# Hedgehog attention plus gated MLP on one core: transposes by DMA in place of TensorE, and a reordered start

## The chip, the cores and the metric

The kernel runs on one core of a Trainium2 chip. The metric is device time in microseconds (us). The core has five engines that run side by side: TensorE (PE, matmuls), VectorE (DVE), ScalarE (ACT), GpSimd (POOL) and SyncE (SP), which here only issues DMA transfers. Matmul results land in PSUM, a small memory of eight banks, and an engine has to copy ("evict") them to SBUF, the on-chip working memory, before they can be a matmul's input again.

## The reference: what is computed

The input x has 2048 rows of 640 in bf16. It is layer-normed once. Two branches use the result and are added to x: a linear attention with 32 heads of 20 columns whose feature map is a softmax of plus and minus a projected q or k ("hedgehog"), and a gated MLP of width 1536.

```python
def _A_ref(x, wqkv, w_phi, wo):
    qkv = (x @ wqkv) ...                              # q, k, v: 32 heads of 20
    pq = jnp.einsum("bhsd,hdf->bhsf", q, w_phi)
    pk = jnp.einsum("bhsd,hdf->bhsf", k, w_phi)
    phi_q = concat([softmax(pq), softmax(-pq)])       # phi_k the same from pk
    kv = jnp.einsum("bhsf,bhsd->bhfd", phi_k, v)
    z  = jnp.einsum("bhsf->bhf", phi_k)
    num = jnp.einsum("bhqf,bhfd->bhqd", phi_q, kv)
    den = jnp.einsum("bhqf,bhf->bhq", phi_q, z)[..., None] + 1e-6
    return (num / den) ... @ wo
def _B_ref(x, w1, w3, w2):
    h = silu(x @ w1) * (x @ w3)
    return h @ w2
xn = _layernorm(x)
return x + _A_ref(xn, ...) + _B_ref(xn, ...)
```

## The kernel before

The 2048 rows are 16 tiles of 128 rows, or 4 chunks of 512. A small planner (`Plan`) takes the operations in the order in which the code lists them, assigns each a guessed duration, and writes out the program in the order of its simulated start. The steps are:

- **LN and T(t)**: layer norm of tile t on DVE, then five PE transposes into a PSUM bank and an evicting copy to `xnT` (columns of x on the partitions).
- **V(t)**, **K(t)**: projections of tile t, ten matmuls of 320 columns each; for K two exponentials (plus and minus), row sums, reciprocal and the two products `phik`.
- **prep**: folds the feature map's weights into wk and wq (`wkphi`, `wqphi`), after transposing these weights on PE.
- **KV(t)**: accumulates kv and z over all tiles in two PSUM banks, `kva` and `kvb`.
- **GU(c, fi)**: one 128-wide slice of gate and up for a chunk (five matmuls of 512 columns each), tanh on ACT, the product `gs` on DVE, and the product `hT` on DVE or on POOL. These units are used as filler between the other steps (`fill`).
- **Q(c, g)**, **RT(t)**, **ATT(pair)**: q for a chunk, numerators and denominators, and the attention output `om` of two tiles.
- **OT(t)** and **O(t)**: transposes `om` on PE, then multiplies hT by w2 and oT by wo into one bank; the residual is added as the bank is evicted.

```python
# ... (cut)
for t in range(4):
    load_x(t, 1)
nc.sync.dma_start(out=wv[:], in_=wqkv3[:, :, 2 * D : 3 * D])
load_gu(0)
nc.sync.dma_start(out=wk[:], in_=wqkv3[:, :, D : 2 * D])
load_x(4, 4)
load_gu(1)
load_x(8, 4)
load_gu(2)
load_gu(3)
nc.sync.dma_start(out=wq[:], in_=wqkv3[:, :, 0:D])
nc.sync.dma_start(out=w2[:], in_=B_w2.rearrange("(c p) d -> p c d", p=P))
# ... (cut)
def T(t, evac="DVE"):
    ln_apply(t)
    # ...
        for c in range(KD):
            nc.tensor.transpose(o["ps"][:, c * P : (c + 1) * P], box["t"][:, c * P : (c + 1) * P], ident[:])
    # ... and the copy
            nc.vector.tensor_copy(out=dst, in_=src)
# ... (cut) prep: transposes, copy, product with wphi
                    for c in range(KD):
                        nc.tensor.transpose(
                            box["ps"][:gw, c * P : (c + 1) * P], src[:, c, 120 * g : 120 * g + gw], ident[:]
                        )
                nc.vector.tensor_copy(out=box["wT"][:gw, :], in_=box["ps"][:gw, :])
                            nc.tensor.matmul(
                                o["ps"][:, c - c0, 0:gw], box["wT"][:gw, c * P : (c + 1) * P], wphi[:gw, g, 0:gw]
                            )
# ... (cut) OT
        for c in range(KD):
            nc.tensor.transpose(o["ps"][:, c * P : (c + 1) * P], box["om", 0][...][:, c * P : (c + 1) * P], ident[:])
        nc.vector.tensor_copy(out=o["oT"][:], in_=o["ps"][:].rearrange("p (c s) -> p c s", c=KD))
# ... (cut) which engine makes hT
def modes(n):
    return "DVE" if n % 3 == 0 else "POOL"
# ... (cut) the second half
RT(0); RT(1); ATT(0); fill(2.2)
for i in range(NST // 2):
    nxt = i + 1
    # RT, ATT of pair nxt, a fill, Q of the next chunk
    OT(2 * i); OT(2 * i + 1)
    O(2 * i); O(2 * i + 1)
```

Of the kernel before, what the change touches and what calls it, by code (L numbers as in the profile page):

```python
# [8 lines left out]
P = 128  # L9


class Plan:
# [7 lines left out]
    def op(self, eng, dur, fn, deps=(), takes=None, frees=(), after=0.0):  # L20
        o = dict(eng=eng, dur=dur, fn=fn, deps=[d for d in deps if d is not None], takes=takes,
                 frees=list(frees), after=after, n=len(self.ops), end=None, open=0)
        for f in o["frees"]:
            f["open"] += 1
        self.ops.append(o)
        return o
# [4 lines left out]
    def run(self):  # L31
# [20 lines left out]
        while left:  # L52
# [14 lines left out]
            o["start"], o["end"] = t, t + o["dur"]  # L67
            free[o["eng"]] = o["end"]
# [7 lines left out]
        for o in out:  # L76
            o["fn"]()
# [3 lines left out]
def kernel(  # L81
# [22 lines left out]
    H = 32  # L104
# [6 lines left out]
    NG = 6  # L111
    GW = [120] * 5 + [40]
    GH = [6] * 5 + [2]
    NQ = 5
    HC = 22
# [16 lines left out]
    xpool = ctx.enter_context(tc.tile_pool(name="xpool", bufs=3))  # L132
    wv, wk, wq = (big.tile([P, KD, D], bf, name=n, tag="big") for n in ("wv", "wk", "wq"))
    xg = {}
    w1 = wpool.tile([P, KD, F], bf, name="w1")
# [4 lines left out]
    wphi = consts.tile([P, NG, P], bf, name="wphi")  # L140
# [5 lines left out]
    kva = kvpool.tile([P, 512], f32, name="kva")  # L146
    kvb = kvpool.tile([P, 512], f32, name="kvb")
# [4 lines left out]
    def load_x(t0, n):  # L152
        i, k = t0 % 4, t0 // 4
        if i == 0:
            xg[k] = xpool.tile([P, 4, D], bf, name="xg", tag="xg")
        nc.sync.dma_start(
            out=xg[k][:, i : i + n, :],
            in_=x2[t0 * P : (t0 + n) * P, :].rearrange("(t p) d -> p t d", p=P),
        )

    def xt(t):
        return xg[t // 4][:, t % 4, :]
# [5 lines left out]
    for t in range(4):  # L168
        load_x(t, 1)
    nc.sync.dma_start(out=wv[:], in_=wqkv3[:, :, 2 * D : 3 * D])  # L170
    load_gu(0)
    nc.sync.dma_start(out=wk[:], in_=wqkv3[:, :, D : 2 * D])
    load_x(4, 4)
    load_gu(1)
    load_x(8, 4)
    load_gu(2)
    load_gu(3)
    nc.sync.dma_start(out=wq[:], in_=wqkv3[:, :, 0:D])
    nc.sync.dma_start(out=w2[:], in_=B_w2.rearrange("(c p) d -> p c d", p=P))

    nc.vector.memset(wphi[:], 0.0)
    for hh in range(6):
        n = len(range(hh, H, 6))
        nc.scalar.dma_start(
            out=wphi[Dh * hh : Dh * hh + Dh, 0:n, Dh * hh : Dh * hh + Dh],
            in_=A_w_phi[hh:H:6].rearrange("g j f -> j g f"),
        )
    ident = consts.tile([P, P], bf, name="ident")
    make_identity(nc, ident[:])
    eps = consts.tile([P, 1], f32, name="eps")  # L190
    nc.vector.memset(eps[:], EPS)
    mhalf = consts.tile([P, NST], f32, name="mhalf")
    nc.vector.memset(mhalf[:], -0.5)
    for v in vaug:
        nc.gpsimd.memset(v[:, :, Dh : Dh + 1], 1.0)

    band = consts.tile([P, 20], bf, name="band")
    nc.gpsimd.memset(band[:], 1.0)
    for lo in (0, 64):
        rows = band[lo : lo + 64, :]  # L200
        nc.gpsimd.affine_select(
            out=rows, in_=rows, pattern=[[-4, 20]], base=16, channel_multiplier=1,
            compare_op=ALU.is_ge, fill=0.0,
        )
        nc.gpsimd.affine_select(
            out=rows, in_=rows, pattern=[[4, 20]], base=3, channel_multiplier=-1,
            compare_op=ALU.is_ge, fill=0.0,
        )
    mask = consts.tile([P, 10, 4], bf, name="mask")
    for j in range(10):  # L210
        b = 4 - (64 * j - Dh * h0[j]) // 4
        nc.gpsimd.tensor_copy(out=mask[:, j, :], in_=band[:, b : b + 16 : 5])
    for kv in kvr:
        nc.gpsimd.memset(kv[:], 0.0)
# [6 lines left out]
    for kv in kvr:  # L221
        for g in range(NQ):
            lo, hi = halves(kv, g)
            nc.gpsimd.tensor_copy(out=lo[:, :, HC - 1], in_=mask[0:64, 2 * g, :])
            nc.gpsimd.tensor_copy(out=hi[:, :, HC - 1], in_=mask[64:128, 2 * g + 1, :])

    plan = Plan(dict(bank=6, row=4, half=2, pair=4, rt=4, th=3, gs=3, up=3, hT=3, big=4, xg=3))
# [13 lines left out]
    arrive = [3.2, 3.6, 4.0, 4.4] + [13.0] * 4 + [19.0] * 8  # L241
    rstd_of = {}
    X_of = {k: plan.alloc("xg", lambda: None) for k in range(3)}
    X_of[3] = plan.op("SP", 0.5, lambda: load_x(12, 4), takes="xg")
    xg_of = dict(X_of)
    big_of = {n: plan.alloc("big", lambda: None) for n in ("wv", "wk", "wq")}
    xn_of = {}
    T_of = {}

    def ln_stats(t):  # L250
        def fn():
            for i in range(2):
                nc.vector.bn_stats(out=stats[:, t, i, :], in_=xt(t)[:, i * 320 : (i + 1) * 320])  # L253
            nc.vector.bn_aggr(out=mv[:, t, :], in_=stats[:, t, :, :])

        return plan.op("DVE", 0.9, fn, after=arrive[t], deps=[X_of.get(t // 4)])

    def ln_rstd(t0, n, pool):
        ds = [ln_stats(t) for t in range(t0, t0 + n)]
        if pool:  # L260

            def fn():
                v = small.tile([P, n], f32, name="vareps", tag=f"vareps{n}")
                nc.gpsimd.tensor_scalar_add(v[:], mv[:, t0 : t0 + n, 1], EPS)
                nc.gpsimd.tensor_tensor(
                    out=rstd[:, t0 : t0 + n], in0=v[:], in1=mhalf[:, 0:n], op=ALU.pow
                )

            r = plan.op("POOL", 1.5, fn, deps=ds)
        else:  # L270

            def fn():
                nc.scalar.activation(
                    out=rstd[:, t0 : t0 + n], in_=mv[:, t0 : t0 + n, 1], func=AF.Sqrt,
                    bias=eps[:, 0:1], scale=1.0,
                )

            a = plan.op("ACT", 0.3, fn, deps=ds)
            r = plan.op(
                "DVE", 0.1,  # L280
                lambda: nc.vector.reciprocal(out=rstd[:, t0 : t0 + n], in_=rstd[:, t0 : t0 + n]),
                deps=[a],
            )
        for t in range(t0, t0 + n):
            rstd_of[t] = r

    def ln_apply(t):
        box = {}

        def al():  # L290
            box["t"] = work.tile([P, D], bf, name="xn", tag="row", bufs=4)

        a = plan.alloc("row", al)

        def fn():
            nc.vector.tensor_scalar(
                out=box["t"][:], in0=xt(t), scalar1=mv[:, t, 0:1], scalar2=rstd[:, t : t + 1],
                op0=ALU.subtract, op1=ALU.mult,
            )

        xn_of[t] = (plan.op("DVE", dve_us(D, 4), fn, deps=[rstd_of[t], a], frees=[xg_of[t // 4]]), a, box)
# [4 lines left out]
    def T(t, evac="DVE"):  # L306
        ln_apply(t)
        dep, xb, box = xn_of[t]
        o = {}

        def fn():
            o["ps"] = bank([P, D], bf)
            for c in range(KD):
                nc.tensor.transpose(o["ps"][:, c * P : (c + 1) * P], box["t"][:, c * P : (c + 1) * P], ident[:])

        u = plan.op("PE", pe_us(KD, P), fn, deps=[dep], takes="bank", frees=[xb])
# [9 lines left out]
        T_of[t] = plan.op(evac, dve_us(D, 2) if evac == "DVE" else act_us(D), ev, deps=[u], frees=[u])  # L326
# [16 lines left out]
    def V(t):  # L343
        V_of[t] = []
        for half in range(2):
            u, o = proj(t, wv, half, [T_of[t]], [big_of["wv"]])
# [11 lines left out]
    def K(t):  # L358
# [11 lines left out]
        for half in range(2):  # L370
            u, o = proj(t, wkphi, half, [T_of[t]] + wphi_ready["k"])
# [10 lines left out]
        def red():  # L382
            box["s"] = small.tile([P, 2, H], f32, name="ks", tag="ks")
# [7 lines left out]
        def rec():  # L391
            box["r"] = small.tile([P, 2, H], f32, name="kr", tag="kr")
            nc.vector.reciprocal(out=box["r"][:], in_=box["s"][:])  # L393
# [3 lines left out]
        def mul(sgn):  # L397
            def fn():
                eng = nc.vector if sgn == 0 else nc.gpsimd
                eng.tensor_mul(  # L400
# [25 lines left out]
    def prep(key, src, dst, after):  # L426
        wphi_ready[key] = []
        units = []
        for g in range(NG):
            gw = GW[g]  # L430
            box = {}

            def tr(g=g, gw=gw, box=box):
                def fn():
                    box["ps"] = bank([P, D], bf)
                    for c in range(KD):
                        nc.tensor.transpose(
                            box["ps"][:gw, c * P : (c + 1) * P], src[:, c, 120 * g : 120 * g + gw], ident[:]
                        )

                def al():
                    box["wT"] = work.tile([P, D], bf, name="wT", tag="half", bufs=2)

                box["al"] = plan.alloc("half", al)
                u = plan.op("PE", pe_us(KD, P), fn, takes="bank", after=after, frees=[big_of["w" + key]])

                def ev():
# [417 lines left out]
```

The softmax here doesn't subtract the row's maximum and nothing guards it: scores larger than these inputs give would overflow.

## Time and profile before

| | before |
|---|---|
| device time, median of 4 runs | 307.31 us (306.32 to 307.86) |
| span of the profiled run | 306.1 us |
| first matmul starts | 7.39 us |
| loads in the first 40 us | about 300 GB/s on average, then almost none |
| HBM read, written | 14.44 MB, 2.62 MB |

How to read it: the page gives busy time by engine, the span in 40 slices (each digit is the busy share of a slice in tenths), and the chain of work that ended last, followed back from the end. Rows of groups name the line, the engine, the operation, "output<-inputs", the shape and the count. An engine's idle time is put down to what released it. A PE that is shown as busy need not run at its peak, because matmuls overlap; their true pace is seen from start to start in the timeline. Some matmul records are missing from the trace, so a count in a row can be a few per cent below the program's.

### The profile page before, as it was taken

The numbers are of one execution on the slowest core, as the hardware profiler recorded it, in microseconds if no ns is written. First come the engines' busy times: TensorE is split into PE (matmuls) and PEld (weight loads), VectorE is DVE, ScalarE is ACT, GpSimd is POOL, SyncE is SP. The second block draws the span as 40 slices with busy tenths as digits, with TensorE's granted clock in tenths as the row PEclk, the third lists the DMA queues.
The fourth block names the chain that finished last, engine by engine and source line by source line (L and its number), as shares of the span: only waits on it lengthen the run. The fifth ranks groups of instructions, "written<-read, shape, count | busy, mean of one in ns | idle before, by whom it ended". The sixth has DMA issues, their size and how long they took to land.

```text
span 306.1 us, 5207 instructions
## 1 busy us (share of the span) xinstructions
PE 282.0 (92%) x2053; PEld 175.3 (57%) x2076; DVE 198.3 (65%) x349; ACT 140.9 (46%) x309; POOL 74.6 (24%) x101
## 2 busy tenths in 40 slices
PE   0768999969999999999999999999998999999995
PEld 0434555526655666656545476665765657657773
DVE  6269699988888776686656944738247372681931
ACT  4135565525555655656488815057060480631100
POOL 8213243253424333354310300011012020120000
PEclk9999999979999999999999999999999999999999
DMA  7999800020003000000300000030000100001011
GB/s 201 349 336 351 290 3 1 0 86 1 0 2 86 2 0 2 2 2 0 109 0 2 0 21 24 6 122 4 22 24 11 34 0 24 21 0 36 9 45 43
DMA packets 16723, 17.39 MB, mean 57 GB/s; under 512 B 1340, under 2 KB 16700, under 8 KB 16700
## 3 DMA queue, kind: packets, MB, share of 16 engines
q1 hardware_dynamic: 16000, 17.04, 17.3%
q8 instruction: 16, 0.26, 0.3%
q10 hardware_dynamic: 700, 0.03, 0.2%
q14 instruction: 7, 0.06, 0.1%
HBM read 14.44 MB, written 2.62 MB: 56 GB/s over the span
## 4 chain that ended last, share of the span: by engine, by line
PE 67%; DVE 16%; issue 6%; DMA 5%; ACT 5%; SPq 1%; POOL 0%; POOLq 0%
PE bank L502 24%; PE bank L738 13%; PE bank L336 10%; PE bank L742 6%; PE bank L590 6%; DVE stats L253 3%; ACT rt L641 3%; DVE gs L523 2%; DMA wv<-in_A_wqkv_dram 2%; DMA xg<-in_A_x_dram 2%; PE bank L633 2%; DVE ks L384 2%; ACT eq L605 2%; DVE phik L400 2%; PE bank L709 1%
## 5 line engine op out<-in xcount | busy, mean ns | idle before, releaser
L502 PE MATMUL bank<-xnT,w 128*128 128x512 bf16 x457 | 109.8, 382 | 5.2 <-DVE xnT L322 2.9
L502 PEld LDWEIGHTS <-w 128*128 128x128 bf16 x480 | 46.9, 98 | 56.0 <-issue 7.1
L545 POOL TENSOR_TENSOR hT<-gs,up 128x512 bf16<-128x512 bf16 x32 | 38.1, 1192 | 157.2 <-DVE gs L523 81.1
L738 PE MATMUL bank<-w,hT 128*128 128x320 bf16 x384 | 57.4, 299 | 0.0
L641 ACT CAST rt<-bank 128x352 bf16<-128x352 f32 x64 | 23.6, 496 | 56.5 <-PE bank L633 47.6
L738 PEld LDWEIGHTS <-hT 128*128 128x128 bf16 x384 | 37.3, 98 | 14.3
L747 DVE TENSOR_TENSOR res<-bank,xg 128x320 bf16<-128x320 f32 x32 | 15.7, 491 | 43.4 <-PE bank L742 43.4
L518 ACT ACTIVATE th<-bank 128x512 bf16<-128x512 f32 x48 | 29.2, 608 | 28.8 <-PE bank L502 27.2
L336 PEld LDWEIGHTS <-xnT 128*128 128x128 bf16 x320 | 30.5, 99 | 19.4 <-DVE xnT L322 5.3
L523 DVE SCALAR_TENSOR_TENSOR gs<-th,bank 128x512 bf16<-128x512 bf16 x48 | 32.3, 675 | 6.7 <-ACT th L518 6.7
L384 DVE TENSOR_REDUCE ks<-ek 128x64 f32<-128x1280 bf16 x16 | 23.7, 1482 | 17.2 <-ACT ek L375 17.2
L400 POOL TENSOR_TENSOR phik<-ek,kr 128x640 bf16<-128x640 bf16 x16 | 24.4, 1528 | 26.0 <-DVE kr L393 23.6
L336 PE MATMUL bank<-wv,xnT 128*128 128x320 bf16 x160 | 25.7, 310 | 5.1 <-DVE xnT L322 3.5
L742 PE MATMUL bank<-wo,oT 128*128 128x320 bf16 x160 | 27.0, 299 | 1.8 <-DVE oT L718 1.8
L375 ACT ACTIVATE ek<-bank 128x320 bf16<-128x320 f32 x64 | 23.1, 435 | 9.3 <-PE bank L336 9.2
L540 ACT ACTIVATE up<-bank 128x512 bf16<-128x512 f32 x32 | 19.1, 597 | 16.8 <-PE bank L502 16.8
L400 DVE TENSOR_TENSOR phik<-ek,kr 128x640 bf16<-128x640 bf16 x16 | 24.6, 1539 | 0.2
L336 PE MATMUL bank<-wkphi,xnT 128*128 128x320 bf16 x160 | 24.4, 299 | 0.0
L349 ACT CAST vaug<-bank 128x320 bf16<-128x320 f32 x32 | 13.7, 428 | 22.0 <-PE bank L336 21.9
L605 ACT ACTIVATE eq<-bank 128x512 bf16<-128x512 f32 x40 | 21.6, 594 | 3.2 <-PE bank L590 3.2
L590 PE MATMUL bank<-xnT,wqphi 128*128 128x512 bf16 x100 | 22.2, 379 | 0.0
L742 PEld LDWEIGHTS <-oT 128*128 128x128 bf16 x160 | 15.5, 98 | 8.4 <-DVE oT L718 2.4
(61 smaller groups left out, 244.1 us busy)
## 6 DMA issues: line engine op xcount, KB each, us to landing
xg<-in_A_x_dram SPq DMA_DIRECT2D x7, 640.0 KB, 7.0
w<-in_B_w_dram SPq DMA_DIRECT2D x8, 480.0 KB, 7.9
out_dram<-res SPq DMA_DIRECT2D x16, 160.0 KB, 1.8
w<-in_B_w_dram SPq DMA_DIRECT2D x1, 1920.0 KB
wv<-in_A_wqkv_dram SPq DMA_DIRECT2D x1, 800.0 KB, 7.1
wk<-in_A_wqkv_dram SPq DMA_DIRECT2D x1, 800.0 KB
wq<-in_A_wqkv_dram SPq DMA_DIRECT2D x1, 800.0 KB, 8.8
wo<-in_A_wo_dram SPq DMA_DIRECT2D x1, 800.0 KB, 4.6
```

What stands on the lines that cost most here:

```text
L336: nc.tensor.matmul(o["ps"][:], xnT[:, c, t * P : (t + 1) * P], w[:, c, 320 * half : 320 * half + 320], start=(c == 0), stop=(c == KD - 1),)
L384: nc.vector.reduce_sum(out=box["s"][:].rearrange("p a h -> p (a h)"), in_=box["ek"][:].rearrange("p a (h d) -> p (a h) d", d=Dh), axis=AX.X,)
L400: eng.tensor_mul(out=phik_b[t][:, :, sgn, :], in0=box["ek"][:, sgn, :].rearrange("p (h d) -> p h d", d=Dh), in1=box["r"][:, sgn, :, None]. ...
L502: nc.tensor.matmul(o["ps"][:], w[:, k, fi * P : (fi + 1) * P], xs[:, k, :], start=(k == 0), stop=(k == KD - 1))
L518: nc.scalar.activation(out=box["th"][:], in_=og["ps"][:], func=AF.Tanh, scale=0.5)
L523: nc.vector.scalar_tensor_tensor(out=box["gs"][:], in0=box["th"][:], scalar=1.0, in1=og["ps"][:], op0=ALU.add, op1=ALU.mult)
L545: lambda: nc.gpsimd.tensor_mul(out=hT[c][:, fi, :], in0=box["gs"][:], in1=box["up"][:]),
L590: nc.tensor.matmul(o["ps"][:], wqphi[:, k, g * P : (g + 1) * P], xnT[:, k, c * 512 : (c + 1) * 512], start=(k == 0), stop=(k == KD - 1),)
L605: nc.scalar.activation(out=eqt[c, sgn][:, g, 0:512], in_=o["ps"][:], func=AF.Exp, scale=1.0 - 2.0 * sgn)
L641: nc.scalar.copy(out=rtt[pair, sgn][:, i, 16 * side : 16 * side + 16, :].rearrange("p h c -> p (h c)"), in_=o["ps"][:],)
L738: nc.tensor.matmul(o["ps"][:], hT[c][:, fi, ti * P : (ti + 1) * P], w2[:, fi, cols], start=(fi == 0), stop=False)
L742: nc.tensor.matmul(o["ps"][:], oo["oT"][:, k, :], wo_of[0][:, k, cols], start=False, stop=(k == KD - 1))
```

## The change

It does several things together.

1. The transposes of xn for chunks 1 to 3, of the k and q weights, and of the attention output are made by DMA (`dma_start_transpose`) and no longer by PE with an evicting copy. [...] xn of a chunk and the attention output of a pair are first stored to a scratch tensor there; the weights are read straight from the input.
2. The start is reordered: x tile by tile with wv in halves between, layer norm per tile, two of the four `xnT` copies on ACT, and the prologue's order fixed by hand. Ten dummy matmuls on zeros (`warm`) run while PE waits for the first data.
3. The phi weights are loaded with one DMA and spread over the block diagonal on POOL; the folding writes three matmuls into one 320-column bank.
4. The product `hT` is on POOL for the first 36 gate/up units, and on DVE for every third after that.
5. x for the residual is loaded again into its own buffers; xn, x, oT and the residual share one pool of four.
6. The attention pairs run two ahead of O instead of one, and half of RT's banks are the two that KV had used.

```diff
@@ loads at the start
+        for t in range(4):
+            load_x(xg[0], t, 1, 0)
+            if t < 2:
+                nc.sync.dma_start(
+                    out=wv[:, :, 320 * t : 320 * t + 320],
+                    in_=wqkv3[:, :, 2 * D + 320 * t : 2 * D + 320 * t + 320],
+                )
+        load_gu(0)
+        load_x(xg[1], 0, 4, 1)
+        nc.sync.dma_start_transpose(out=wkT[:], in_=A_wqkv[:, D : 2 * D])
+        for i in range(1, 4):
+            load_gu(i)
... (cut)
+    def warm():
+        nc.vector.memset(xnT[:, 0, 0:512], 0.0)
+        ps = bank([P, 512], f32)
+        for i in range(WARM):
+            nc.tensor.matmul(ps[:], xnT[:, 0, 0:P], xnT[:, 0, 0:512])
+    WARM = 10
... (cut) layer norm of chunks 1 to 3
+        st = plan.op(
+            "SP", 0.5,
+            lambda: nc.sync.dma_start(out=xn_d[c][:].rearrange("(t p) d -> p t d", p=P), in_=xn[c][:]),
+            deps=ds, frees=[a], lat=3.5,
+        )
+        xt = plan.op(
+            "SP", 0.5,
+            lambda: nc.sync.dma_start_transpose(out=xnT[:, :, 512 * c : 512 * c + 512], in_=xn_d[c][:]),
+            deps=[st], lat=5.0,
+        )
... (cut) prep
-                        nc.tensor.transpose(
-                            box["ps"][:gw, c * P : (c + 1) * P], src[:, c, 120 * g : 120 * g + gw], ident[:]
-                        )
-                    nc.vector.tensor_copy(out=box["wT"][:gw, :], in_=box["ps"][:gw, :])
+                    for n, (g, at, width, col) in enumerate(FSPANS[side]):
+                        nc.tensor.matmul(
+                            o["ps"][:, at : at + width], wT[:, g, c * P : (c + 1) * P],
+                            wphi[:, g, :, :].rearrange("p i f -> p (i f)")[:, col : col + width], ...
... (cut) OT
-                nc.tensor.transpose(o["ps"][:, c * P : (c + 1) * P], box["om", 0]..., ident[:])
-            nc.vector.tensor_copy(out=o["oT"][:], in_=o["ps"][:].rearrange("p (c s) -> p c s", c=KD))
+            lambda: nc.sync.dma_start(
+                out=o_d[pair][:].rearrange("(t p) d -> p t d", p=P),
+                in_=box["om", 0][:].rearrange("p (t h) d -> p t (h d)", t=2),
+            ),
+            deps=[dep], frees=[ob], lat=2.5,
+            lambda: nc.sync.dma_start_transpose(out=oT[c][:, :, 256 * i : 256 * i + 256], in_=o_d[pair][:]),
+            deps=[st, oT_a[c]], lat=3.5,
... (cut)
     def modes(n):
-        return "DVE" if n % 3 == 0 else "POOL"
+        return "DVE" if n % 3 == 0 and n >= 36 else "POOL"
... (cut) after the start; wqT and w2 are held back to these times of the plan
+    plan.op("SP", 0.5, lambda: nc.sync.dma_start_transpose(out=wqT[:], in_=A_wqkv[:, 0:D]), after=24.0)
+    LN(1)
+    plan.op("SP", 0.5, lambda: nc.sync.dma_start(out=w2[:], ...), after=36.0)
... (cut) the second half
+    residual(0)
+    attend(0, 2.2)
+    attend(1, 2.2)
     for i in range(NST // 2):
-        nxt = i + 1
+        nxt = i + 2
```

## The prediction, made before the changed kernel ran

> **What bounds the kernel now.** I read the busy line and the 40 slices first, to see which engine fills the span and where it doesn't.
>
> ```profile
> PE 282.0 (92%) x2053; PEld 175.3 (57%) x2076; DVE 198.3 (65%) x349; ACT 140.9 (46%) x309; POOL 74.6 (24%) x101
> PE   0768999969999999999999999999998999999995
> DVE  6269699988888776686656944738247372681931
> ```
>
> TensorE (PE) is at 9 in nearly every slice after the fifth. So the kernel is a stream of matmuls with a slow start, and two questions remain: how dense that stream is, and what the start costs. Next, the timeline of PE alone over the first 22 us (start, duration, count, and in brackets the idle time before):
>
> ```profile
> 7.39 0.71 PE L314 MATMUL bank<-ident,xn 128*128 128x128 bf16 x5 [7.39 <-DVE xn L296]
> 9.75 2.82 PE L336 MATMUL bank<-wv,xnT 128*128 128x320 bf16 x10 [1.65 <-DMA wv<-in_A_wqkv_dram]
> 13.69 1.53 PE L336 MATMUL bank<-wv,xnT 128*128 128x320 bf16 x10 [0.59 <-DVE xnT L322]
> 17.69 1.53 PE L336 MATMUL bank<-wv,xnT 128*128 128x320 bf16 x10 [2.19 <-DVE xnT L322]
> 20.20 1.53 PE L336 MATMUL bank<-wv,xnT 128*128 128x320 bf16 x10 [0.69 <-DVE xnT L322]
> 21.57 4.48 PE L502 MATMUL bank<-xnT,w 128*128 128x512 bf16 x19
> ```
>
> The gate/up matmuls (L502) begin only at 21.57 us. Until then PE has done four transposes of five and four V projections of ten; it waited for layer norm, for wv, and for the copies of xnT. The first V group takes 2.82 us and the later ones 1.53.
>
> The table by stage (columns: stretch, its length, then busy us and count for PE, PEld, DVE, ACT, POOL, then PE clock, DMA share, GB/s) shows the middle:
>
> ```profile
> 40.00:65.00 25.00, 21.79 (x149) 12.55 (x150) 24.46 (x34) 13.89 (x33) 11.48 (x11) 0.98 0.01 1
> 65.00:154.00 89.00, 88.38 (x670) 54.08 (x681) 66.39 (x83) 50.42 (x115) 34.80 (x27) 0.99 0.08 25
> 154.00:303.00 149.00, 145.99 (x1062) 93.41 (x1066) 81.24 (x161) 59.85 (x130) 13.55 (x11) 1.00 0.07 22
> ```
>
> From 40 to 65 us VectorE (DVE) is busy 24.46 of 25: there it is the bound. The chain of work that ended last says the same; from 38 to 64 us it runs mostly over DVE:
>
> ```profile
> 42.24 1.49 DVE ks L384
> 43.73 0.59 DVE gs L523
> 44.70 0.63 DVE hT L532
> 45.33 1.55 DVE phik L400
> ```
>
> After 65 us PE is full. In the waits of PE only two lines belong there:
>
> ```profile
> PE bank L502 <- DVE xnT L322: 2.9, 1, 2.9
> PE bank L742 <- DVE oT L718: 1.8, 2, 1.2
> ```
>
> **What the Trainium skill says.** "TensorE: Matmul & The Clock Gate", section "Back-to-back issue gap", gives about N/2.4 + 2.5 ns per warm matmul of N columns. The trace agrees: the timeline has 10 matmuls of 512 in 2.16 us (216 ns each), 10 of 320 in 1.36, 10 transposes of 128 in 0.56. Section "What's actually happening" says the clock is halved until the array has been busy for some 3.4 us; the first V group at 2.82 us against 1.53 fits that. "DMA: Bandwidth & Descriptors", section "Latency and other measured facts", gives 261 GB/s for one transposing DMA; no such DMA is in this trace. "VectorE: DVE Perf Modes", section "The three transpose paths", gives 1309 ns for one 128x128 block by DMA against 390 on TensorE. If the blocks ran one after another that would be 25 GB/s. These two disagree tenfold in what they imply; this is my main uncertainty.
>
> **PE's work, counted.** From the program, by the trace's pace: 580 matmuls of 512 x 0.216 = 125.3 us; 864 of 320 x 0.136 = 117.5; 220 transposes x 0.056 = 12.3; 60 for folding phi x 0.054 = 3.2; 192 of the attention (24 in 1.40 us, 0.058) = 11.2; 160 of kv x 0.038 = 6.1. Sum 275.6 of 306.1. The other 30.5 us: 7.4 before the first matmul; 3.3 after the last (302.84 to 306.1); and about 20 in between, which I place with the counted work of each stretch: some 14 before 65 us, 6 after.
>
> **The change, part by part.**
> 1. *Transposes leave PE.* Tiles 4 to 15 of xn (12 x 5), both weights (60) and the attention output (80) now go by DMA: 200 x 0.056 = 11.2 us off PE, all of it inside a full stream, so I count it fully. The folding of phi stays at 60 matmuls of the same mean width: 0. PE's work becomes 264.4 us, not counting the ten warming matmuls.
> 2. *The start.* x arrives tile by tile with wv in halves between, layer norm goes per tile, and ScalarE takes two of the four xnT copies. DVE per tile: stats 0.86, reciprocal 0.13, apply 0.40 (0.80 for two), and two copies of 0.47 in all; from 2.93 us, when x arrives, that is 4 x 1.39 + 0.94 = 6.5, plus about 0.5 for hops: xnT of tile 3 at about 10 us. V(2) and V(3) follow, so gate/up starts at about 12.7 instead of 21.57. PE's work up to there is the same 6.6 us, so 8.9 us are saved. Ten dummy matmuls from 1.3 us fill the wait and take the cold pace (2.82 - 1.53 = 1.3 us) off the first group; this is inside the 8.9.
> 3. *DVE is relieved* in the stretch where it bounds: 14 of 16 copies of xnT go (12 with their transposes, 2 to ScalarE; 14 x 0.48 = 6.7), 12 wT copies (5.6), 12 of 16 hT products go to POOL (12 x 0.65 = 7.8), and later 16 oT copies (7.1). DVE goes from 198 to about 171. From gate/up's start to the last K tile I count for DVE 32 gs x 0.675 + 16 x (1.48 + 0.54 + 1.54) + 12 stats x 1.05 + 12 applies x 0.6 = 98 us, beside PE's 32 x 2.16 + 16 K and 12 V x 1.36 + 16 kv x 0.38 + 3.2 = 116: DVE is no longer the bound, though at 85% it still makes PE wait here and there. ACT takes 12 more up copies (7.2) and POOL 12 x 1.19 = 14.3; both are under 60%. Of the 14 us lost from 7.4 to 65 us about 7.5 fall before 21.57 (14.2 less 6.6 of work), which part 2 covers, and 6.5 after; I let 4 remain.
> 4. *New waits.* xn of a chunk is stored to DRAM, then read back transposed. The plan's own figures are 3.5 + 5 us for 640 KB and 2.5 + 3.5 for 320 KB. For chunk 1: apply ends near 21 us; the queue then still holds about 2 MB of weights (loads ran at 345 GB/s), store lands near 29, transpose near 37. PE needs it after 12 gate/up units and four K: 12.7 + 12 x 2.16 + 3.2 / 2 + 4 x 1.36 + 0.8 = 46. Hidden with 9 us to spare. wkT: about 3 MB lie ahead of it, so it starts near 11.5 us and lands near 15; PE asks at 12.7 + 3 x 2.16 = 19.2. Hidden. For the first attention output: from the last matmul of tile 1 to the use, PE has two gate/up units, six attention groups of 0.84 less two, one Q of 5.4 and 12 matmuls: 4.3 + 3.4 + 5.4 + 1.6 = 14.7 us. The chain is rt copies 2, coefficients 2.1, products and sum 3.9, a gs 0.7, store and transpose 6, hops 1: 15.7. About 1 us of stall. The two waits above (2.9, 1.8) go away.
>
> Sum: 264.4 work + 6.1 before gate/up (12.7 - 6.6) + 4 to 65 us + 4 after + 3.3 tail = 281.8. I add 3 us for transposing DMAs slower than the plan's figures and for waits in SP's queue, which is in order. The timed median is about 1.2 over the profiled span (307.31 against 306.1). Together: 286 us.
>
> **Rivals.**
> - *The transposing DMA is slow.* At 100 GB/s (8 us for 800 KB) wkT and the second weight chunk come 2 us late and chunk 1 about 2: near 290. At 25 to 50 GB/s wkT would land at 28 or later, the weights queued behind it with it, and xn of chunk 1 some 10 us late: 304 to 315. Against it: the one stated bandwidth, and the plan's figures. For it: the 1309 ns.
> - *DVE stays the bound to 140 us.* If the 1.5 us products and reductions grow further because POOL now has 44 instead of 32 multiplications beside them, the K stage runs at DVE's pace: 98 us x 1.18 = 116, as much as PE has; order waits would then cost some 5 to 8 us, giving 291 to 294.
> - *SP's queue blocks.* Stores, transposes, residual loads and output stores stand in one order, and each issue waits for its own producer. An output store waiting for DVE in front of a transpose would show as PE waiting on oT; 1 to 2 us a time, four times, near 291.
> - *All hidden, better start.* Gate/up from 11.5 us and hardly a wait: 278.
>
> **Range and chances.** 278 is the hidden case, 297 holds the milder rivals together. Slower than 301 needs a really slow transpose. 278 to 297; faster 0.91, same 0.06, slower 0.03.
>
> **What will show it.** Right: no L314-style transposes on PE but 20; first gate/up near 12.7 us; DVE under 90% from 40 to 65; PE's waits on DMA xnT, wkT and oT under 3 us in total; transposing DMAs landing in 3 to 6 us. Wrong: PE waiting on DMA wkT or xnT for many us (first rival); PE waiting on DVE gs or phik through the K stage (second); PE waiting on oT at each pair (third).

## The result, and the profile after

The changed kernel takes 281.72 us (median; 280.72 to 284.24), the kernel before 307.84 in the same series: ratio 0.9169, 95% interval 0.9143 to 0.9194. (The ratio is taken over all runs and is not the quotient of the two medians.) The prediction was 286.0 with a range of 278 to 297.

The page of the changed kernel, busy line and slices:

```profile
PE 269.6 (97%) x1862; PEld 163.3 (58%) x1886; DVE 172.5 (62%) x295; ACT 145.9 (52%) x320; POOL 95.7 (34%) x124
PE   6799999999999999999999999999999999999994
DVE  4683789979767666857629976223664706647221
```

PE is at 9 from the third slice on, and no 8 is left in the middle. Its first 6 is mostly the dummy matmuls, so "97% busy" flatters it a little. The timeline of PE over the start:

```profile
1.24 4.18 PE L210 MATMUL bank<-xnT 128*128 128x512 bf16 x10 [1.24 <-DVE xnT L207]
5.55 0.45 PE L377 MATMUL bank<-ident,xn 128*128 128x128 bf16 x5
7.00 1.53 PE L399 MATMUL bank<-wv,xnT 128*128 128x320 bf16 x10 [1.01 <-DVE xnT L385]
9.37 0.45 PE L377 MATMUL bank<-ident,xn 128*128 128x128 bf16 x5 [0.84 <-DVE xn L327]
...
12.58 2.89 PE L399 MATMUL bank<-wv,xnT 128*128 128x320 bf16 x20
15.30 6.64 PE L548 MATMUL bank<-xnT,w 128*128 128x512 bf16 x29
```

Gate/up (L548) begins at 15.30 us, against 21.57 before. The first V group takes 1.53 us instead of 2.82, as every later one does. The table by stage, with the same columns as before:

```profile
40.00:65.00 25.00, 24.84 (x168) 14.22 (x170) 23.14 (x36) 15.41 (x33) 16.20 (x14) 1.00 0.36 122
65.00:140.00 75.00, 74.12 (x531) 44.07 (x539) 53.02 (x85) 50.47 (x112) 42.00 (x31) 1.00 0.18 47
140.00:276.00 136.00, 134.81 (x954) 85.61 (x960) 70.71 (x123) 55.18 (x123) 13.14 (x11) 1.00 0.24 67
```

From 40 to 65 us PE is now busy 24.84 of 25 (21.79 before). DVE still has 23.14, but PE no longer waits for it. The waits of PE over the whole span, less the four of the start (3.8 us together), are two lines:

```profile
PE bank L548 <- DVE gs L569: 0.4, 1, 0.4
PE rtbank L682 <- ACT rt L690: 0.2, 1, 0.2
```

No DMA stands among them. Only the weight loads (PEld), which overlap PE, waited 0.4 us for one, a transposed attention output (the last entry of the row):

```profile
L794 PEld LDWEIGHTS <-oT 128*128 128x128 bf16 x160 | 15.5, 98 | 6.4 <-DMA oT<-od 0.4
```

All transposing transfers of this kernel read DRAM: the scratch tensors `xnd` and `od`, and the weights in the input. Here they are with the stores in front of them, in the DMA view (count, size if given, median us from issue to landing):

```profile
od<-om SPq DMA_DIRECT2D x8, 320.0 KB, 2.3
xnd<-xn SPq DMA_DIRECT2D x3, 640.0 KB, 3.2
...
oT<-od SPq DMA_TRANSPOSE x8, 3.6
xnT<-xnd SPq DMA_TRANSPOSE x3, 4.8
...
wkT<-in_A_wqkv_dram SPq DMA_TRANSPOSE x1, 9.7
wqT<-in_A_wqkv_dram SPq DMA_TRANSPOSE x1, 10.6
```

**Where the time went.** By the prediction's count PE's work is 275.6 us before and 264.4 after, so 30.5 us of the span before (306.1) and 14.8 of the span after (279.2) are without work. The balance closes on the span's 26.9 us:

| us | before | after | change |
|---|---|---|---|
| PE's counted work | 275.6 | 264.4 | -11.2 |
| without work ahead of gate/up (start of gate/up less 6.6 of work) | 15.0 | 8.7 | -6.3 |
| without work between that and the last matmul (the rest) | 12.2 | 2.5 | -9.7 |
| after the last matmul (302.8 and 275.6) | 3.3 | 3.6 | +0.3 |

Of the 9.7 us, 6.0 are waits: PE's list before names 6.6 us after the start of gate/up (2.9, 1.8, 0.9, 0.8 and 0.2), the list now 0.6. Another 1.3 us went by at a low clock behind the longest of these waits; the section on the rule for hT shows it. The rest is not placed.

The balance says where time was saved, not which part of the change saved it. The experiments undo one part at a time.

### The profile page after: what moved, and what is told of

Same layout as the page of the kernel before. It is cut to its first block, busy times and chain, and to the rows that moved or that the text cites. A ratio compares the mean times of both kernels' runs of the same rounds, so it can differ in the third digit from the quotient of the medians.

```text
span 279.2 us, 4872 instructions
## 1 busy us (share of the span) xinstructions
PE 269.6 (97%) x1862; PEld 163.3 (58%) x1886; DVE 172.5 (62%) x295; ACT 145.9 (52%) x320; POOL 95.7 (34%) x124
## 2 busy tenths in 40 slices
DMA packets 44614, 26.54 MB, mean 95 GB/s; under 512 B 26288, under 2 KB 44592, under 8 KB 44592
## 4 chain that ended last, share of the span: by engine, by line
PE 85%; issue 4%; ACT 4%; DVE 2%; DMA 2%; POOL 1%; SPq 1%; ACTq 0%; POOLq 0%
PE bank L548 35%; PE bank L790 17%; PE bank L399 14%; PE bank L794 7%; PE bank L636 6%; PE rtbank L682 2%; DMA xg<-in_A_x_dram 2%; ACT eq L651 2%; PE bank L682 2%; PE bank L505 1%; PE kva L481 1%; PE kvb L481 1%; ACT rt L690 1%; POOL phik L464 1%; DVE xn L327 1%
## 5 line engine op out<-in xcount | busy, mean ns | idle before, releaser
L548 PE MATMUL bank<-xnT,w 128*128 128x512 bf16 x460 | 109.7, 379 | 1.5 <-DVE gs L569 0.4
L591 POOL TENSOR_TENSOR hT<-gs,up 128x512 bf16<-128x512 bf16 x44 | 51.3, 1166 | 141.7 <-ACT up L586 84.0
L548 PEld LDWEIGHTS <-w 128*128 128x128 bf16 x480 | 46.3, 98 | 49.4 <-issue 0.7
L790 PE MATMUL bank<-w,hT 128*128 128x320 bf16 x384 | 58.1, 299 | 0.0
L586 ACT ACTIVATE up<-bank 128x512 bf16<-128x512 f32 x44 | 26.3, 597 | 23.3 <-PE bank L548 21.7
L447 DVE TENSOR_REDUCE ks<-ek 128x64 f32<-128x1280 bf16 x16 | 23.6, 1475 | 17.4 <-ACT ek L438 17.4
L464 POOL TENSOR_TENSOR phik<-ek,kr 128x640 bf16<-128x640 bf16 x16 | 29.7, 1856 | 5.5 <-ACT th L564 5.5
L799 DVE TENSOR_TENSOR res<-bank,xr 128x320 bf16<-128x320 f32 x32 | 15.5, 486 | 25.4 <-PE bank L794 25.4
L690 ACT CAST rt<-bank 128x352 bf16<-128x352 f32 x32 | 13.1, 469 | 26.4 <-PE bank L682 18.8
L399 PE MATMUL bank<-wv,xnT 128*128 128x320 bf16 x160 | 24.4, 299 | 1.8 <-DVE xnT L385 1.0
L464 DVE TENSOR_TENSOR phik<-ek,kr 128x640 bf16<-128x640 bf16 x16 | 21.9, 1366 | 1.4
L636 PEld LDWEIGHTS <-wqphi 128*128 128x128 bf16 x100 | 9.6, 98 | 10.8
```

The source lines that it names most:

```text
L399: nc.tensor.matmul(o["ps"][:], xnT[:, c, t * P : (t + 1) * P], w[:, c, 320 * half : 320 * half + 320], start=(c == 0), stop=(c == KD - 1),)
L447: nc.vector.reduce_sum(out=box["s"][:].rearrange("p a h -> p (a h)"), in_=box["ek"][:].rearrange("p a (h d) -> p (a h) d", d=Dh), axis=AX.X,)
L464: phik_ins[t] = eng.tensor_mul(out=phik_b[t][:, :, sgn, :], in0=box["ek"][:, sgn, :].rearrange("p (h d) -> p h d", d=Dh), in1=box["r"][:, ...
L548: nc.tensor.matmul(o["ps"][:], w[:, k, fi * P : (fi + 1) * P], xs[:, k, :], start=(k == 0), stop=(k == KD - 1))
L586: nc.scalar.activation(out=box["up"][:], in_=ou["ps"][:], func=AF.Copy, scale=0.5)
L591: lambda: nc.gpsimd.tensor_mul(out=hT[c][:, fi, :], in0=box["gs"][:], in1=box["up"][:]),
```

## The experiments

Ratios are to the kernel before; the changed kernel's is 0.9169. A step of 0.01 is 3.1 us. Most intervals are about 0.004 to each side, 1.2 us, and the changed kernel's own is 0.0025; a difference of two ratios is therefore known to about 1.5 us to each side. Three single runs that were several us slower than the rest of their kernel (292.21, 289.63 and 311.76 us) are not in the ratios.

| edit of the changed kernel | median us | ratio, 95% interval | against 0.9169, us |
|---|---|---|---|
| no dummy matmuls | 283.51 | 0.9223 (0.9182 to 0.9265) | +1.7 |
| attention output transposed on PE | 288.50 | 0.9390 (0.9353 to 0.9427) | +6.8 |
| xn tiles 4 to 15 transposed on PE | 285.56 | 0.9305 (0.9272 to 0.9338) | +4.2 |
| hT by the old rule | 281.00 | 0.9169 (0.9136 to 0.9203) | 0 |
| k weights transposed on PE | 282.50 | 0.9195 (0.9164 to 0.9227) | +0.8 |
| prologue's order left to the scheduler | 287.70 | 0.9350 (0.9311 to 0.9389) | +5.6 |
| all of x ahead of wv | 283.45 | 0.9219 (0.9177 to 0.9260) | +1.5 |
| three kinds of transposes on PE | 294.40 | 0.9610 (0.9569 to 0.9651) | +13.6 |
| ten more dummies | 281.03 | 0.9157 (0.9124 to 0.9190) | -0.4 |
| x tile 2 sooner | 281.54 | 0.9180 (0.9144 to 0.9217) | +0.3 |
| both, and x tile 1 sooner | 281.51 | 0.9163 (0.9127 to 0.9199) | -0.2 |
| *the kernel before* with the new rule for hT | 304.60 | 0.9918 (0.9889 to 0.9946) | |

### Attention output transposed on PE

```diff
-        ATT(pair); OT(pair)                  # store, then transposing DMA
+        ATT(pair)
+        OT(i)                                # just ahead of O: 10 PE transposes, 2 DVE copies
         O(2 * i); O(2 * i + 1)
```

> The changed kernel with the 80 transposes of the attention output back on PE (and 16 copies on DVE), just ahead of O. Count theory: PE is full in this half, so it costs 80 x 0.056 = 4.5 us: about 286.2 us, ratio 0.931. Rival, hidden gain: with pairs running two ahead, the DMA way has waits of its own that PE's way hasn't, and the cost is under 2.5 us. Second rival: DVE's 16 copies add waits, over 6.5 us.

It costs more than the count, just above the line at which I had said DVE's copies add waits. The waits of PE in this run carry a line that the changed kernel lacks:

```profile
PE bank L799 <- DVE oT L772: 2.0, 2, 1.5
```

4.5 us of transposes and 2.0 of waits make 6.5 of the 6.8. So this transfer removed two things: matmul slots, and a hop PE to DVE to PE just ahead of O. (The profiled run is not a typical one: its gate/up also began 1.0 us late, at 16.29, and it took 289.10 us against the median of 288.50.) In the changed kernel that hop is a store and a DMA that start when `om` is ready, two pairs ahead; only the 0.4 us of weight load above waited for it. The 2.0 us belong to transposes placed just ahead of O, as in the kernel before (1.8). Transposes on PE that come a pair earlier were not tried; they might have kept part of this gain.

### xn tiles 4 to 15 transposed on PE

```diff
-        st = ... dma_start(out=xn_d[c] ...); xt = ... dma_start_transpose(out=xnT[...], in_=xn_d[c][:])
+        # in the K loop: T(4) to T(7) at t = 0 to 3, T(8) to T(15) at t = 6 to 13, copies on DVE
```

> The changed kernel with the 60 transposes of xn tiles 4 to 15 back on PE (and 12 copies on DVE), spread over the K stage. Count theory: 60 x 0.056 = 3.4 us: about 285.1, ratio 0.928. Rival, DVE theory: DVE is busy 23.1 of 25 us from 40 to 65 us already; 12 copies of 0.48 bring it back to being the bound, and the cost is 6 us or more, with PE waiting on DVE gs, xnT or phik.

The count gives 3.4, and one wait of PE on a copy of xnT adds 1.2:

```profile
PE bank L536 <- DVE xnT L373: 1.2, 1, 1.2
```

Measured were 4.2, known to about 2.9 to 5.5. This fits the count theory with one wait. The DVE rival (6 us or more) falls: with twelve copies more, PE waits on gs for only 0.2 us.

### k weights transposed on PE

```diff
-        nc.sync.dma_start_transpose(out=wkT[:], in_=A_wqkv[:, D : 2 * D])
+        nc.sync.dma_start(out=wk[:], in_=wqkv3[:, :, D : 2 * D])
+    # 25 PE transposes and 5 DVE copies between the first gate/up units
```

> The changed kernel with the k weights loaded straight and transposed by 25 PE transposes (and 5 copies on DVE); the q weights stay on DMA. Count theory: 25 x 0.056 = 1.4 us slower, 283.1. Queue theory: the transposing DMA of the k weights held SP's queue for 7.65 us and landed 9.7 us after its issue; without it the weights behind it land some 5 us sooner, but no wait of PE for them was seen, so that brings nothing. Rival: the early DVE (layer norm of chunk 1) is pushed back by the copies, and the cost is 3 us or more.

The cost is 0.8 us, with an interval that holds 1.4 and also 0: it agrees with the count and does not prove it. In the profiled run PE also waited 0.6 us for wk to arrive. The queue theory's premise is seen in the changed kernel's SP timeline:

```profile
6.04 7.65 SPq L179 DMA_TRANSPOSE wkT<-in_A_wqkv_dram x1
13.74 5.38 SPq L163 DMA_DIRECT2D w<-in_B_w_dram x6
```

Issuing this one transfer takes SP 7.65 us, and the next six weight loads stand behind it. In the changed kernel PE doesn't wait for them (its list has no such line), so freeing the queue brought nothing that was seen.

### Three kinds of transposes on PE

The three edits above together; only the q weights stay on DMA.

> The changed kernel with the transposes of the attention output (80), of xn tiles 4 to 15 (60) and of the k weights (25) all back on PE; the start stays as changed, and the q weights stay on DMA. Count theory: 165 x 0.056 = 9.2 us more, 291. Additivity: one at a time they cost 6.8, 3.8 and 0.8 us, 11.4 together: 293, ratio 0.954. Rival: the transposes off PE are nearly the whole gain and together cost far more than singly, because DVE gets all 33 copies back: 296 or more.

The cost is 13.6 us, against 11.8 for the sum of the three ratios. The intervals of the four allow a sum without interaction; they don't exclude 1 or 2 us of it. Count and seen waits give 9.2 + 2.0 + 1.2 = 12.4. The rival of a far larger cost together (296 us or more, over 14 us) is not met. Part of the 13.6 is the start and not the transposes: in the profiled run (296.61 us) the granted clock, the part of full speed that PE was allowed, was 0.72 from 4 to 15 us, and the V projections ended some 2.7 us late, at 18.03. The four runs with a mean clock near 1.0 took 293.77 to 294.71 us, 12.0 to 13.0 above the changed kernel's median.

### The prologue's order left to the scheduler

```diff
-    with tc.manual_schedule(engines={ET.PE, ET.DVE, ET.Activation, ET.Pool, ET.SP}):
+    if True:
```

> The changed kernel with the prologue left to the scheduler, not fixed by hand. Order theory: part of the 6.3 us won before gate/up (21.57 to 15.30) is the order on DVE and ACT (layer norm of later tiles ahead of copies that PE waits for); without it gate/up starts 1 to 4 us later, and the time is up by as much. Rival: the loads and the per-tile layer norm make the gain, and the time stays within 0.7 us.

The cost is 5.6 us, more than the 1 to 4 expected. Gate/up begins at 20.46 us, 5.2 later than with the fixed order and only 1.1 earlier than in the kernel before. PE's timeline has the wait and the late start:

```profile
10.40 0.71 PE L377 MATMUL bank<-ident,xn 128*128 128x128 bf16 x5 [5.28 <-DVE xn L327]
...
20.46 3.83 PE L548 MATMUL bank<-xnT,w 128*128 128x512 bf16 x16
```

and DVE's timeline the reason:

```profile
4.22 0.21 DVE L289 BATCH_NORM_AGGREGATE mv<-stats 128x2 f32<-128x12 f32 x1
6.29 0.89 DVE L286 BATCH_NORM_STATS2 stats<-xg 128x6 f32<-128x320 bf16 x2 [1.86 <-DMA xg<-in_A_x_dram]
...
9.91 0.78 DVE L327 TENSOR_SCALAR xn<-xg,mv,rstd 128x640 bf16<-128x640 bf16 x2
```

The statistics of tile 0 are done at 4.43 us, but its normalised rows come at 9.91, because the scheduler put the statistics of three later tiles in front, and DVE, in order, also waited for x tile 1. In the fixed order that step starts at 5.04. After the wait the first V group was at the cold pace again (2.85 us), in spite of the dummies, so a small part of the cost may be the clock.

### No dummy matmuls, and more of them

```diff
-    WARM = 10
+    WARM = 0
```

> The changed kernel without the ten dummy matmuls. Clock theory: the first transposes and V groups run at the cold pace, as the first V group of the kernel before did (2.82 against 1.53 us), and gate/up starts about 1 to 1.5 us later than 15.30: ratio to the kernel before 0.920 to 0.922 instead of 0.917. Rival, waits theory: before 11.3 us PE waits for layer norm and for x anyway, so a slow first group is hidden in these waits, and the time stays within 0.5 us of the changed kernel's.

The cost is 1.7 us in the ratio, but known only to about 0.2 to 3.2. In the profiled run the first V group is at the cold pace (2.81 us) and gate/up starts at 15.90, 0.6 late. The slow group took 1.3 us longer, so in this run part of it hides in waits, as the rival has it, and 0.6 us don't.

```diff
+    T(0, "DVE");  keep(4)      # keep(n): n dummy matmuls of 512 columns on zeros
+    V(0);         keep(3)
+    T(1, "ACT");  keep(3)
```

> The changed kernel with ten more dummy matmuls, four after the first transposes, three after V(0), three after the transposes of tile 1, where PE waits in the start. Clock theory: the changed kernel's runs spread from 280.7 to 284.2, and in those above 284 the granted clock was 0.988 instead of 0.997 to 1.0; the clock falls in these early waits. Filled, the median goes to 281.0 and the spread closes to about 1 us. Rival: the dummies hold up the transposes and V behind them on PE, and gate/up starts up to 0.7 us later, 282.4; or the spread has another cause and stays.

The runs lie in 280.70 to 281.88, against 280.72 to 284.24, as the clock theory had it (a median of 281.0 and a spread of about 1 us). But the medians can't be told apart, and with six and eleven runs a narrower spread is an indication only. In the profiled run gate/up began at 16.25 us, not earlier. The profiled run of the variant with the attention output on PE shows what may be behind the spread: its first V group took 2.85 us again, with the ten early dummies in place, and the granted clock (third number from the end) had fallen:

```profile
6.00:9.00 3.00, 1.57 (x6) 0.89 (x7) 2.27 (x7) 0.29 (x1) 2.92 (x12) 0.73 1.08 334
9.00:12.00 3.00, 2.22 (x13) 1.39 (x12) 2.30 (x10) 1.92 (x5) 2.54 (x12) 0.70 1.28 336
```

### The order of the first loads

The changed kernel loads x0, wv's first half, x1, wv's second half, x2, x3. Three other orders:

```diff
 # all of x first       x0 x1 x2 x3 wv0 wv1
 # x tile 2 sooner      x0 wv0 x1 x2 wv1 x3
 # both                 x0 x1 wv0 x2 wv1 x3, and dummies keep(4), keep(1), keep(4)
```

> The changed kernel with all four x tiles loaded before the two halves of wv. The start of the changed kernel waits for x tile 2, which landed at 7.65 us behind the wv halves, and its DVE idled 0.73 us for it. If x bounds the start, gate/up comes 0.5 to 1 us earlier: 280.9. Rival: V(0) then waits for wv, as in the kernel before (9.75 us), and it is 0.5 to 2 us slower.

> The changed kernel with the second half of wv loaded after x tile 2 instead of before it. If the landing of x tile 2 (7.65 us, with DVE idle 0.73 us for it) sets the start, gate/up begins about 0.5 us earlier and DVE's idle time goes: 281.2. Rival: V(0) then waits for the second half of wv, as with all of x first, and it is 0.3 to 1 us slower; or ScalarE's copies, not DVE, set the start, and nothing moves.

> The changed kernel with both remedies for the start: loads in the order x0, x1, first half of wv, x2, second half of wv, x3, and nine dummy matmuls where PE waits (four after the transposes of tile 0, one after V(0), four after the transposes of tile 1). In the run with ten dummies DVE waited 1.35 us for x tile 1, which lay behind wv, and gate/up began at 16.25; with x2 sooner it began at 14.69. If the start's landing times and the clock are all that still varies, gate/up begins at 14.7 or before, every run lies within 1 us, and the median is 280.4, ratio 0.913 to 0.915. Rival: V(0) now waits for wv, and it is 281 to 282, as the two alone.

With all of x first, PE waits for wv instead:

```profile
PE bank L399 <- DMA wv<-in_A_wqkv_dram: 1.9, 1, 1.9
```

That wait alone is not what the order costs. In this profiled run (284.51 us) the clock was 0.74 from 4 to 15 us, five V matmuls behind the wait took 1.5 us instead of 0.85, and gate/up began at 18.84. Four of the six runs had a mean clock of 0.987 to 0.994 and took 282.94 to 284.92 us; the two with 1.0 took 281.20 and 282.22. So the 1.5 us come mostly with a low clock; whether the order brings the low clock is not shown.

With x2 sooner, gate/up begins at 14.69 in the profiled run, 0.6 earlier, and DVE's wait for x2 is gone, yet the median doesn't move. With all remedies the expectation of 280.4 failed: 281.51. The runs are close together (280.76 to 281.71), as expected, but V(0) waits 0.6 us for wv's second half and gate/up begins at 15.26. No variant is shown to be faster than the changed kernel.

### The rule for hT, alone and undone

```diff
-        return "DVE" if n % 3 == 0 and n >= 36 else "POOL"
+        return "DVE" if n % 3 == 0 else "POOL"
```

> The changed kernel with hT on DVE for every third gate/up unit from the start, as before. DVE theory: 12 products of 0.65 us more on DVE, of which some 5 fall before 65 us; DVE's 23.1 of 25 us there can't take 3 us more, so 2 to 4 us are lost, 284 to 286. Rival: these products and POOL's work beside them slow each other down (POOL's phik went from 1.53 to 1.86 us), and the old rule costs nothing, within 1 us.

> The kernel before with only the new rule for hT (POOL for the first 36 units). DVE theory: before 65 us DVE bounds the kernel before (24.46 busy of 25 us), and 4 or 5 products of 0.65 us fewer there are worth 2 to 3 us: 305, ratio 0.990 to 0.993. Rival: it is the other work (layer norm, copies, K) that bounds, and the time stays within 1 us.

The same rule is worth 2.5 us (1.7 to 3.4) in the kernel before and nothing in the changed one. PE's timeline shows where the 2.5 us lie. The kernel before:

```profile
64.94 3.63 PE L502 MATMUL bank<-xnT,w 128*128 128x512 bf16 x9 [2.86 <-DVE xnT L322]
68.40 1.52 PE L336 MATMUL bank<-wv,xnT 128*128 128x320 bf16 x10
```

and with the new rule alone:

```profile
63.55 2.32 PE L502 MATMUL bank<-xnT,w 128*128 128x512 bf16 x9 [1.53 <-DVE xnT L322]
65.71 1.52 PE L336 MATMUL bank<-wv,xnT 128*128 128x320 bf16 x10
```

It is one wait, for a copy of xnT that in the kernel before starts on DVE at 64.41, behind a `phik` (62.41) and a `gs` (63.81). The wait falls from 2.86 to 1.53 us. In addition, the ten gate/up matmuls behind it took 3.46 us from start to start before, and 2.16 with the rule: the granted clock was 0.50 from 65 to 67 us before, and 1.00 with the rule. That is 1.3 + 1.3 = 2.6 us, the whole gain. The second part is not in every run of the kernel before: in this series four of its thirteen runs had a mean clock of 1.0 (spans of 303.4 to 305.2 us), the others 0.994 (305.0 to 306.8).

In the changed kernel this copy has left DVE, and DVE's high share from 40 to 65 us cost PE nothing. With the old rule put back:

```profile
40.00:65.00 25.00, 25.00 (x171) 14.23 (x170) 23.35 (x38) 13.62 (x30) 12.23 (x11) 1.00 0.34 118
```

PE is full beside a DVE that is busy for 23.35 of 25 us. One wait was relieved twice over.

## Why the prediction was right, point by point

- **Transposes leave PE** (11.2 us, counted fully): held. Three of the four kinds, put back together, cost 13.6 where the count gives 9.2; of the excess, 2.0 and 1.2 are seen as waits on the copies, and a low clock in the start of two runs is part of the rest. The q weights weren't tried. One term of the count was a little small: the folding does not keep its mean width (40 matmuls of 140 columns and 20 of 80, against 50 of 120 and 10 of 40), and the 30 for k took 1.89 us, 0.063 each instead of 0.054. So PE's work after is some 0.5 us more than 264.4, and what is left without work as much less.
- **The start** (gate/up at 12.7): right kind, too early by 2.6 us. My DVE sum ended at about 10 us; the last copy of xnT ended at 13.2. A tile's layer norm took 1.6 us instead of 1.39, x tile 2 landed at 7.65 us, so that DVE idled 0.73 for it, and the last copy waited 1.31 for PE. DVE's timeline has the wait for x tile 2, the late rows of tile 1 and the late copy:

```profile
7.68 0.89 DVE L286 BATCH_NORM_STATS2 stats<-xg 128x6 f32<-128x320 bf16 x2 [0.73 <-DMA xg<-in_A_x_dram]
...
8.87 0.45 DVE L327 TENSOR_SCALAR xn<-xg,mv,rstd 128x640 bf16<-128x640 bf16 x1
...
12.74 0.49 DVE L385 COPY xnT<-bank 128x640 bf16<-128x640 bf16 x1 [1.31 <-PE bank L377]
```

  The normalised rows of tile 1 (8.87) stand behind the statistics of tile 2 (7.68) even in the order fixed by hand, and PE waits 0.8 us for them; no run moved them. I also credited the loads in pieces and the layer norm per tile. With these and the dummies, but without the fixed order, gate/up began only 1.1 us earlier than before; the order adds 5.2. The order without the new loads was not tried.
- **DVE relieved** (4 us left to 65, 4 after): too cautious by 5.5 us. After 15.30 us only about 2.5 remain without work, and waits of 0.6 are named. DVE at 93% did not hold PE up, although I had named a share under 90% as a sign of being right and let 85% still make PE wait: I had taken a high share for waits. I had also misread the kernel before there. The wait of 2.9 us lies before 65 us, not after (62.08 to 64.94), and PE, "full" after 65, was at half clock up to about 68; so this copy of xnT cost 4.2 us and not 2.9.
- **New waits**: hidden, as said. xn of chunk 1 landed at 31.87 + 5.1 = 37.0 us, as predicted, and its first use, K of tile 4, is at 49.28. That the time agrees is luck: the store was issued only at 27.88, after SP had spent 8.60 us on issuing wqT, and landed some 3 us later than I had said, and the transpose was as much faster than the 8 us I had left for it. wkT landed at 15.7 (predicted 15) and was used at 21.78. The first attention output was the tight one: predicted 1 us of stall, measured 0.4.
- **The allowance of 3 us** for slow transposes and SP's queue wasn't needed, though the sign "landing in 3 to 6 us" was missed: wkT and wqT took 9.7 and 10.6, and one oT 6.8.
- **The sum**, on the span: 284.8 predicted (281.8 + 3) + 2.6 (start) - 5.5 (middle) - 3 (allowance) + 0.3 (tail) = 279.2, as measured. The errors partly cancelled: the number is closer than its parts.
- **Rivals**: the slow transpose came half true and harmless: wkT was slower than the 100 GB/s of the milder case, and PE did not wait for it. wkT reached 84 GB/s from issue to landing (819,200 bytes in 9.7 us), xnT 137 (655,360 in 4.8). In the Trainium skill, "DMA: Bandwidth & Descriptors", section "Latency and other measured facts", has 261 GB/s, which none of these reached with their latency counted in; the 1309 ns a block of "VectorE: DVE Perf Modes", section "The three transpose paths", would have made wkT 33 us, by an estimate of 25 blocks one after another. DVE as the bound, and SP's queue, did not show.
- **The pace of a matmul**: the section "Back-to-back issue gap" of "TensorE: Matmul & The Clock Gate" in the Trainium skill gives the formula that I used for an isolated matmul, and for streams of weight load and matmul it states 81 ns at 128 columns and 131 at 512. The streams of this trace kept the formula's pace (56 and 216 ns), so the count stands on the trace.

**What stays open.** The undone parts sum to some 19 us (13.6 transposes with their waits, 5.6 order) of 25.6. The dummies (1.7, wide interval), the q weights, the attention two pairs ahead with its extra banks, and how these overlap make the remaining 6; I have not separated them.

## What to carry to other kernels

In this kernel, with PE full, each matmul slot that DMA took over was worth about its pace in full, and taking out a PE, copy, PE hop was worth its wait as well; DMA could do the transposes with hardly a wait, issued a stage ahead as they were. In a start that waits on several engines, look at the order of instructions on the in-order engine first: here it was worth more than the order of the loads. A high busy share is a bound only while another engine is seen to wait for it; once that wait was gone, the next relief of the same engine was worth nothing. And look at PE's pace behind a wait, too: a busy PE at half clock looks full.

## What the runs showed of the hardware that I had not expected

- Issuing a transposing DMA occupies SP for long: 7.65 and 8.60 us for 25 blocks of 128x128 with strided source rows (wkT, wqT), 2.70 for 20 blocks (xnT) and 1.33 for 10 (oT); a plain transfer of this kernel took 0.35 to 1.15. Per block wkT and wqT are over twice the others; whether this is the strided source or the busy queue was not tried. Packets under 512 bytes went from 1,340 to 26,288: the 6.2 MB transposed are about 250 bytes a packet.
- The POOL half of `phik` got slower as POOL was given more, while its code stayed the same. The page before:

```profile
L400 POOL TENSOR_TENSOR phik<-ek,kr 128x640 bf16<-128x640 bf16 x16 | 24.4, 1528 | 26.0 <-DVE kr L393 23.6 <-ACT th L518 2.4
```

and after:

```profile
L464 POOL TENSOR_TENSOR phik<-ek,kr 128x640 bf16<-128x640 bf16 x16 | 29.7, 1856 | 5.5 <-ACT th L564 5.5
```

  The mean goes from 1528 to 1856 ns, as in the kernel before with the new rule for hT alone (1850), while the DVE half falls from 1539 to 1366. POOL no longer waits for DVE's `kr` (23.6 us before, none in the row after), so the two halves run less side by side; what each competes with was not tried.
- The granted clock fell in the middle of a kernel: to 0.50 from 65 to 67 us in the kernel before, behind a wait of 2.86 us, and to 0.73 from 6 to 9 us in the run shown above, whose ten dummy matmuls ended at 4.90. A wait of this size did not always bring it: behind 2.19 us of waiting in the kernel before, the V group at 17.69 us still took 1.53. The mean clock of the changed kernel's runs ranges from 0.987 to 1.0; where it fell in those was not recorded.
- The cold pace at the very start does not show in the clock column: without the dummies the first V group took 2.81 us (7.29 to 10.10), while the column has 1.00 from 6 to 12 us.
